# Moving four late modulation products and their weight loads from a block of their own into the attention-value loop, and storing the `ga` row as bf16

## The chip, the cores and the metric

The kernel runs on one core of one Trainium2 chip. The metric is the device time of one execution in microseconds (us). It was timed repeatedly. The profile is taken of one execution; its span is about 1.7 us shorter than that execution's time (773.4 against 775.11 us before).

Engines: PE does matmuls, PEld its weight loads, DVE is the vector engine, ACT the scalar engine, POOL the general one; SP only issues DMAs here. SBUF is the on-chip memory that holds the tiles, PSUM the one that PE writes its products to; a DMA is a transfer to or from DRAM.

## The reference, cut to what matters

An adaptive layer-norm transformer block, with 2048 tokens of width 1024. A conditioning vector `c` gives six modulation vectors; a sliding, dilated local attention (8 keys per query, 32 heads) and an MLP with mish activation follow.

```python
mod = (_silu(c) @ w_mod).reshape(c.shape[0], 6, 1, -1)      # w_mod: 1024 x 6144
sa, ca, ga, sb, cb, gb = (mod[:, i].copy() for i in range(6))
h = _layernorm(x) * (1 + ca) + sa
x = x + ga * _A_ref(h, A_wqkv, A_wo)       # local attention, then @ wo
h = _layernorm(x) * (1 + cb) + sb
x = x + gb * _B_ref(h, B_w1, B_b1, B_w2)   # MLP: 1024 -> 3584 -> 1024
```

`ca` and `sa` are wanted at the very start. `ga` is wanted when the attention output meets `wo`, `cb` and `sb` at the second layer norm, and `gb` only at the end. These four are the "late" vectors; their weights are 8 loads of 1 MB.

## The kernel before

Three stages: (1) Q and K projections, logits and softmax, token chunk by token chunk; the softmax weights (`attn`) go to DRAM. (2) For each of 32 items (4 chunks x 8 column blocks): project V (`emit_v`, PE), multiply by the softmax weights and half-sum (`emit_pv`, DVE), finish the sum with identity matmuls (`emit_osum`, PE). When a chunk is complete, multiply by `wo` (`emit_wo`, PE) and add the residual. (3) The MLP. The late modulation stood between (1) and (2), in what I call the seam:

```python
def emit_mod(i, late=False):
    j = mod_order[i]
    for e in range(NE):                                  # two halves of 512 columns
        ...
        mp = psum.tile([P, EC], FP32, name="mp", tag="mm", bufs=4)
        for kt in range(ND):                             # 8 matmuls; all 128 rows of mp are alike
            nc.tensor.matmul(mp[:], lhsT=silu_bc[:, kt, :], rhs=wm[:, kt, :], ...)
        if j in (SA, CA, SB_, CB):                       # take the diagonal: one value per partition
            ...
            nc.vector.tensor_mul(out=tmp[:, 0:NT, :], in0=mp[:]..., in1=ident[:]...)
            nc.vector.tensor_reduce(out=modT[:, j, ...], in_=tmp[:, 0:NT, :], axis=AX.X, op=ALU.add)
        elif j == GA:                                    # fold ga into the columns of wo
            row = wV.tile([P, EC], FP32, name="row", tag="x1", bufs=3)
            nc.vector.tensor_copy(out=row[:], in_=mp[:])
            for t in range(ND):
                nc.vector.tensor_mul(out=wo_sb[:, t, e * EC:(e + 1) * EC],
                                     in0=wo_sb[:, t, e * EC:(e + 1) * EC], in1=row[:])
        else:
            nc.vector.tensor_copy(out=gb_bc[:, e * EC:(e + 1) * EC], in_=mp[:])
...
workA.__exit__(None, None, None)          # stage 1's tiles (attn among them) give their memory up
...                                       # stage 2's pools (wV) take it
for k0 in range(n_first, n_hb, n_late_bufs):             # two rounds of four 1 MB loads
    for k in range(k0, min(n_hb, k0 + n_late_bufs)):
        nc.sync.dma_start(late_buf(k), wm_src(k))
    for k in range(k0, min(n_hb, k0 + n_late_bufs)):
        if (k - n_first) % NE == 0:
            emit_mod(k // NE, late=True)                 # GA, CB, then SB_, GB
... # first w1 loads, on the ACT queue

def emit_pv(ch, cb):
    for hf in range(NHALF):                              # two halves
        ...
        nc.vector.tensor_mul(out=pv, in0=attnB, in1=vwin)                        # 128x2048
        ... nc.vector.tensor_add(out=pv[:, :, 0:n, :], in0=..., in1=...)         # 128x1024
...
for it in range(n_items + 3):
    if it < n_items:
        ...
        emit_v(ch, cb)
    if 1 <= it <= n_items:
        emit_pv(*divmod(it - 1, ND))
    if 2 <= it <= n_items + 1:
        emit_osum(...)
    ...                                                  # emit_wo for chunk 0 from it = 10
```

The builder reorders what the program emits, engine by engine, so the order that runs is not quite the order of the text.

## Time and profile before

| kernel before | |
|---|---|
| timed | 776.07 us (median of 4 runs, 775.11 to 776.63) |
| span of the profile | 773.4 us |
| Q/K stage, then the seam, up to the first `wo` product | 0 to 239.15 us |
| first `wo` product to the end | 534.25 us |

The page of the kernel before opens with its span and each engine's busy time (share of the span, number of instructions):

```profile
span 773.4 us, 13166 instructions
## 1 busy us (share of the span) xinstructions
PE 718.9 (93%) x5297; PEld 439.2 (57%) x5378; DVE 571.0 (74%) x1004; ACT 446.1 (58%) x882; POOL 1.8 (0%) x9
```

PE looks like the only limit. That is an average, though. The timeline of DVE in the seam of the kernel before (columns: start us, length us, engine, line, operation, output <- inputs, count, and in brackets the idle time before it and what ended it):

```profile
176.79 1.29 DVE L352 TENSOR_REDUCE mx<-L_ps 128x128 f32<-128x512 f32 x2 [1.22 <-PE L_ps L339]
...
180.85 1.91 DVE L361 TENSOR_REDUCE sm<-Lsb 128x128 f32<-128x1024 f32 x1 [1.12 <-ACT Lsb L359]
182.79 0.95 DVE L362 RECIPROCAL sm<-sm 128x128 f32<-128x128 f32 x1
183.78 1.23 DVE L364 TENSOR_TENSOR attn<-Lsb,sm 128x1024 bf16<-128x1024 f32 x1
188.69 1.29 DVE L246 COPY row<-mp 128x512 f32<-128x512 f32 x2 [3.69 <-DMA attn_dram<-attn]
189.90 9.71 DVE L248 TENSOR_TENSOR arena<-arena,row 128x512 bf16<-128x512 bf16 x16
199.53 1.28 DVE L241 TENSOR_TENSOR diag_tmpL<-mp,ident 128x512 f32<-128x512 f32 x2
...
207.89 2.36 DVE L447 TENSOR_TENSOR arena<-attnB,vT 128x2048 bf16<-128x2048 bf16 x2 [1.65 <-ACT vT L434]
210.16 1.28 DVE L451 TENSOR_TENSOR arena<-arena 128x1024 bf16<-128x1024 bf16 x2
211.37 2.35 DVE L447 TENSOR_TENSOR arena<-attnB,vT 128x2048 bf16<-128x2048 bf16 x2
```

This is a serial chain. (`row` is the `ga` vector, copied out of PSUM; L246 is line 246 of the kernel.) The softmax of the last chunk runs until 185.0 us. DVE then stands 3.69 us idle until `attn` has landed in DRAM, because the first tile of stage 2 (`row`) takes memory that `attn` held. After that come the GA copies and 16 multiplies of `wo` (9.71 us), the diagonals, the `gb` copies. Only at 207.89 us does the first attention-value product (L447) start; from there an item takes about 3.48 us (207.89 to 211.37) with no idle. PE in the same seam, kernel before:

```profile
189.44 3.11 PE L233 MATMUL mp<-arena,silu_bc 128*128 128x512 bf16 x8 [3.29 <-DVE row L246]
...
200.26 2.72 PE L233 MATMUL mp<-arena,silu_bc 128*128 128x512 bf16 x6 [5.32 <-DVE diag_tmpL L241]
203.20 2.31 PE L233 MATMUL mp<-arena,silu_bc 128*128 128x512 bf16 x9 [0.22 <-issue]
205.34 5.34 PE L432 MATMUL mp<-hTv,arena 128*128 128x512 bf16 x24
...
239.15 0.38 PE L480 MATMUL mp<-arena,oT 128*128 128x512 bf16 x1
```

PE's modulation products (L233) wait for PSUM buffers that DVE frees, and the V projections (L432) come after all of them. The first `wo` product (L480) starts at 239.15 us. Between the last Q x K product on DVE (173.2 us) and that point, the table of stretches of the kernel before has (busy us of each engine, number of instructions, granted clock, DMA share and rate):

```profile
core 0: us, PE busy (x) PEld busy (x) DVE busy (x) ACT busy (x) POOL busy (x), PEclk, DMA share, GB/s
173.20:239.15 65.95, 47.62 (x248) 25.81 (x253) 57.62 (x75) 15.00 (x43) 0.00 (x0) 0.92 0.70 224
```

DVE works 57.62 of 65.95 us and idles 8.33; PE has 18 us to spare. So DVE is taken to be the limit of this stretch; after it, the same table has PE busy 519.11 of 534.25 us, so there PE is the limit. Lastly two lines of the table of groups of the kernel before (busy us, mean ns of one):

```profile
L451 DVE TENSOR_TENSOR arena<-arena 128x1024 bf16<-128x1024 bf16 x64 | 41.1, 682 | 0.0
L248 DVE TENSOR_TENSOR arena<-arena,row 128x512 bf16<-128x512 bf16 x16 | 9.7, 682 | 0.0
```

A multiply of `wo` with an fp32 `row` takes 682 ns for 512 elements; an all-bf16 add takes as long for twice as many.

### The profile page before, as it was taken

The numbers are of one execution on the slowest core, as the hardware profiler recorded it, in microseconds if no ns is written. First come the engines' busy times: TensorE is split into PE (matmuls) and PEld (weight loads), VectorE is DVE, ScalarE is ACT, GpSimd is POOL, SyncE is SP. The second block draws the span as 40 slices with busy tenths as digits, with TensorE's granted clock in tenths as the row PEclk, the third lists the DMA queues.
The fourth block names the chain that finished last, engine by engine and source line by source line (L and its number), as shares of the span: only waits on it lengthen the run. The fifth ranks groups of instructions, "written<-read, shape, count | busy, mean of one in ns | idle before, by whom it ended". The sixth has DMA issues, their size and how long they took to land.

```text
span 773.4 us, 13166 instructions
## 1 busy us (share of the span) xinstructions
PE 718.9 (93%) x5297; PEld 439.2 (57%) x5378; DVE 571.0 (74%) x1004; ACT 446.1 (58%) x882; POOL 1.8 (0%) x9
## 2 busy tenths in 40 slices
PE   2999999986779999999999999999999999999997
PEld 1444444442345555565677666767676666667653
DVE  3798875756899594951599978778777877778752
ACT  4387565430143879552489796685866757464520
POOL 0000000000000000000000000000000000000000
PEclk9999999998999999999999999999999999999999
DMA  9974212129913646159900312121020101101011
GB/s 325 369 286 164 70 56 69 56 62 319 321 54 115 219 153 195 63 171 300 345 1 25 94 29 88 42 76 42 21 69 28 35 28 35 42 21 42 22 48 48
DMA packets 52519, 87.90 MB, mean 114 GB/s; under 512 B 3690, under 2 KB 31338, under 8 KB 50794
## 3 DMA queue, kind: packets, MB, share of 16 engines
q1 hardware_dynamic: 44602, 75.52, 29.2%
q10 hardware_dynamic: 7856, 11.54, 4.4%
q8 instruction: 42, 0.69, 0.4%
q14 instruction: 19, 0.16, 0.1%
HBM read 69.22 MB, written 17.83 MB: 113 GB/s over the span
## 4 chain that ended last, share of the span: by engine, by line
PE 58%; DVE 23%; ACT 10%; DMA 5%; issue 3%; SPq 0%; DVEq 0%; another core or an unknown queue 0%; ACTq 0%
PE mp L585 22%; PE h L559 20%; DVE arena L447 6%; PE mp L312 6%; DVE arena L327 4%; PE mp L480 3%; DVE arena L451 3%; DMA xin<-in_A_x_dram 2%; DVE bn_st L150 2%; PE mp L233 2%; ACT ee L571 2%; PE mp L432 1%; DMA xres<-in_A_x_dram 1%; DVE arena L248 1%; ACT ee L572 1%
## 5 line engine op out<-in xcount | busy, mean ns | idle before, releaser
L559 PE MATMUL h<-h2T,arena 128*128 128x256 bf16 x1792 | 205.2, 273 | 0.3 <-DVE hm L564 0.2
L585 PE MATMUL mp<-arena,actT 128*128 128x512 bf16 x863 | 193.1, 379 | 2.4 <-DVE actT L576 0.6
L559 PEld LDWEIGHTS <-arena 128*128 128x128 bf16 x1792 | 174.3, 98 | 28.4 <-issue 2.4
L585 PEld LDWEIGHTS <-actT 128*128 128x128 bf16 x896 | 87.4, 98 | 99.5 <-DVE actT L576 1.8
L564 DVE TENSOR_SCALAR hm<-h,b1m 128x256 bf16<-128x256 f32 x224 | 99.6, 477 | 32.5 <-PE mp L483 21.2
L312 PE MATMUL mp<-hT,arena 128*128 128x512 bf16 x483 | 116.1, 379 | 2.1 <-issue 0.5
L571 ACT ACTIVATE ee<-ee,two_t 128x512 f32<-128x512 f32 x112 | 80.0, 716 | 44.4 <-DVE ee L570 44.3
L569 ACT ACTIVATE ee<-bigB 128x512 f32<-128x512 bf16 x112 | 69.0, 618 | 57.5 <-DVE bigB L567 56.7
L576 DVE SCALAR_TENSOR_TENSOR actT<-ee,hm 128x512 bf16<-128x512 f32 x112 | 76.9, 688 | 28.0 <-ACT ee L572 27.6
L327 DVE TENSOR_TENSOR arena<-qT,kT 128x2048 bf16<-128x2048 bf16 x64 | 75.6, 1212 | 28.7 <-ACT kT L317 28.7
L570 DVE SCALAR_TENSOR_TENSOR ee<-ee 128x512 f32<-128x512 f32 x112 | 76.8, 687 | 25.3 <-ACT ee L569 25.1
L447 DVE TENSOR_TENSOR arena<-attnB,vT 128x2048 bf16<-128x2048 bf16 x64 | 75.3, 1217 | 19.0 <-ACT vT L434 19.0
L312 PEld LDWEIGHTS <-arena 128*128 128x128 bf16 x512 | 47.0, 98 | 51.8 <-issue 0.7
L572 ACT ACTIVATE ee<-ee 128x512 f32<-128x512 f32 x112 | 69.7, 624 | 1.9
L432 PE MATMUL mp<-hTv,arena 128*128 128x512 bf16 x245 | 61.1, 379 | 0.5
L480 PE MATMUL mp<-arena,oT 128*128 128x512 bf16 x251 | 60.5, 379 | 0.3
L432 PEld LDWEIGHTS <-arena 128*128 128x128 bf16 x256 | 36.0, 144 | 16.0
L434 ACT CAST vT<-mp 128x512 bf16<-128x512 f32 x32 | 18.7, 586 | 45.1 <-PE mp L432 43.0
L462 PE MATMUL op<-arena,ident 128*128 128x256 bf16 x256 | 35.9, 273 | 7.7 <-DVE arena L451 6.5
L480 PEld LDWEIGHTS <-oT 128*128 128x128 bf16 x256 | 25.0, 98 | 28.9 <-issue 2.4
L451 DVE TENSOR_TENSOR arena<-arena 128x1024 bf16<-128x1024 bf16 x64 | 41.1, 682 | 0.0
L233 PE MATMUL mp<-arena,silu_bc 128*128 128x512 bf16 x93 | 27.4, 451 | 11.0 <-DVE diag_tmpL L241 5.3
(81 smaller groups left out, 555.5 us busy)
## 6 DMA issues: line engine op xcount, KB each, us to landing
arena<-in_w_mod_dram SPq DMA_DIRECT2D x8, 1024.0 KB, 7.3
x_dram<-x SPq DMA_DIRECT2D x32, 256.0 KB, 3.0
x1c<-x_dram SPq DMA_DIRECT2D x16, 512.0 KB, 3.7
bigB<-x_dram SPq DMA_DIRECT2D x32, 256.0 KB, 3.0
arena<-in_B_w_dram ACTq DMA_DIRECT2D x7, 1024.0 KB, 6.7
arena<-in_B_w_dram SPq DMA_DIRECT2D x4, 1792.0 KB, 9.2
xin<-in_A_x_dram SPq DMA_DIRECT2D x16, 256.0 KB, 6.2
arena<-in_w_mod_dram SPq DMA_DIRECT2D x2, 2048.0 KB, 11.2
```

The source lines that it names most:

```text
L312: nc.tensor.matmul(mp[:], lhsT=wqk_sb[:, which, kt, cb * P:(cb + 1) * P], rhs=hT[:, kt, :], start=(kt == 0), stop=(kt == ND - 1))
L327: nc.vector.tensor_mul(out=prod, in0=qT[:, hf * SH:(hf + 1) * SH].unsqueeze(1).to_broadcast([P, W, SH]), in1=_ap(kT[:, HALO + hf * SH:HALO ...
L432: nc.tensor.matmul(mp[:], lhsT=wqk_sb[:, 2, kt, bass.ds(cb, P, step=ND)], rhs=hTv[:, kt, :], start=(kt == 0), stop=(kt == ND - 1))
L447: nc.vector.tensor_mul(out=pv, in0=attnB, in1=vwin)
L480: nc.tensor.matmul(mp[:], lhsT=oT[:, cb, b * P:(b + 1) * P], rhs=wo_sb[:, cb, e * EC:(e + 1) * EC], start=(cb == 0), stop=False)
L559: nc.tensor.matmul(mp[:, i, :], lhsT=w1_sb[:, ft // 4, kt, (ft % 4) * P:(ft % 4 + 1) * P], rhs=h2T[:, kt, :], start=(kt == 0), stop=(kt == ...
L564: nc.vector.tensor_scalar(out=hm2[:, i, :], in0=mp[:, i, :], scalar1=-2.0, scalar2=b1m2[:, ft:ft + 1], op0=ALU.mult, op1=ALU.add)
L570: nc.vector.scalar_tensor_tensor(out=ee[:], in0=ee[:], scalar=2.0, in1=ee[:], op0=ALU.add, op1=ALU.mult)
L571: nc.scalar.activation(out=ee[:], in_=ee[:], func=ACT.Ln, bias=two_t[:], scale=1.0)
L572: nc.scalar.activation(out=ee[:], in_=ee[:], func=ACT.Exp, scale=-1.0)
L576: nc.vector.scalar_tensor_tensor(out=halves[ft0 // NFH][:, ft0 % NFH:ft0 % NFH + 2, :], in0=ee[:], scalar=0.5, in1=hm2[:], op0=ALU.subtrac ...
L585: nc.tensor.matmul(mp[:], lhsT=actT_of(ch, ft)[:, b * P:(b + 1) * P], rhs=w2_sb[:, ft, e * EC:(e + 1) * EC], start=(ft == 0), stop=(ft == ...
```

## The change

Its intent is to hide the weight loads and the modulation products behind the V loop: the four late vectors are emitted one by one in loop steps 1, 2, 4 and 5, their loads in steps 0 and 3, and the first `w1` loads in step 6. `row` becomes bf16 and moves to another ring (the buffers that tiles of one `tag` take in turn).

```diff
-                row = wV.tile([P, EC], FP32, name="row", tag="x1", bufs=3)
+                row = wV.tile([P, EC], BF16, name="row", tag="xres", bufs=3)
...
-    for k0 in range(n_first, n_hb, n_late_bufs):
-        for k in range(k0, min(n_hb, k0 + n_late_bufs)):
-            nc.sync.dma_start(late_buf(k), wm_src(k))
-        for k in range(k0, min(n_hb, k0 + n_late_bufs)):
-            if (k - n_first) % NE == 0:
-                emit_mod(k // NE, late=True)
...
+    late_sched = {}
+    n_late_vec = (n_hb - n_first) // NE
+    vec_per_round = max(1, n_late_bufs // NE)
+    itc = 0
+    for v0 in range(0, n_late_vec, vec_per_round):
+        vecs = list(range(v0, min(n_late_vec, v0 + vec_per_round)))
+        late_sched.setdefault(itc, []).append(("load", vecs))
+        for vv in vecs:
+            itc += 1
+            late_sched.setdefault(itc, []).append(("mod", vv))
+        itc += 1
+    late_sched.setdefault(itc, []).append(("w1", None))
+    def emit_late(it): ...      # emits the loads, emit_mod(2 + vv, late=True) or the w1 loads of this step
...
-    for it in range(n_items + 3):
+    for it in range(max(n_items + 3, max(late_sched) + 1)):
         ch, cb = divmod(it, ND)
+        emit_late(it)
```

More of the change, by code (lines that the diff above doesn't have):

```diff
@@ L396, with emit_late @@
     wV = workV.__enter__()
-    for k0 in range(n_first, n_hb, n_late_bufs):
-        for k in range(k0, min(n_hb, k0 + n_late_bufs)):
-            nc.sync.dma_start(late_buf(k), wm_src(k))
-        for k in range(k0, min(n_hb, k0 + n_late_bufs)):
-            if (k - n_first) % NE == 0:
-                emit_mod(k // NE, late=True)
     w1_v = B_w1.rearrange("(t p) (g n) -> p g t n", p=P, n=EC)
     n_early = min(NG1, (2 * ND * D) // (ND * EC))
-    for g1 in range(NG1):
-        if g1 < n_early or g1 * ND * EC >= NQK:
-            nc.scalar.dma_start(w1_sb[:, g1], w1_v[:, g1])
+    late_sched = {}
[10 more added lines that the diff above has]
+    late_sched.setdefault(itc, []).append(("w1", None))
+    def emit_late(it):
+        for kind, arg in late_sched.get(it, []):
+            if kind == "load":
+                for vv in arg:
+                    for e in range(NE):
+                        k = n_first + vv * NE + e
+                        nc.sync.dma_start(late_buf(k), wm_src(k))
+            elif kind == "mod":
+                emit_mod(2 + arg, late=True)
+            else:
+                for g1 in range(NG1):
+                    if g1 < n_early or g1 * ND * EC >= NQK:
+                        nc.scalar.dma_start(w1_sb[:, g1], w1_v[:, g1])
     oT_tiles = {}
```

## The prediction

> **What bounds the kernel now.** PE is busy 93% of the span (engine table), and 287.5 of the 289 us from 450 to 739. The change touches one seam, between the last Q/K projection (172.5 us) and the first attention-value product (L447, 207.9 us). In the table of stretches, 168 to 206 us has PE 25.4, DVE 28.5, ACT 3.3 of 38 us. The timeline shows a serial chain on DVE: last softmax (176.8 to 185.0), 3.7 us of waiting for the attn write to DRAM, then 188.7 to 206.2 the GA row copies (1.3), 16 multiplies of wo (9.7), diagonal extraction and gb copies. PE's mod products wait for PSUM buffers that DVE frees (5.3 and 3.3 us). V projections come after all of them, so the first pv starts 1.65 us after DVE has run dry. Then items 0 to 8 of the V loop are DVE-bound at 3.475 us each, until wo joins at 239.2 us and PE is the limit (76.9 of 80 us).
>
> **What the change does.** The built order shows V0 ahead of the mod products, pv of items 0 and 1 inside the last softmax, GA after attn, then CB; SB after pv 2, gb after pv 3; from pv 5 on every engine has the order of before. So only the seam can change, and what counts is DVE time from 173.2 us to the end of pv 8.
>
> 1. DVE idle filled: 1.2 (before mx), 1.1 (before sm), 0.5 (gb), 1.65 (first pv): 4.5 us.
> 2. The row becomes bf16. The Trainium skill, "VectorE: DVE Perf Modes", walkthrough of mode 2x_1P, asks 16-bit operands for two results a cycle. Trace: L248 with an fp32 row takes 682 ns for 512 elements (0.607 us start to start); L451, all bf16, 682 ns for 1024 (0.60). I estimate 415 ns, 0.34 us start to start: 16 times 0.27 = 4.3 us less.
> 3. Not removed: the built row copy still waits for the DMA lanes of the attn write (landing 3.7 us); only one add (0.6 us) stands between attn and it. About 3 us of idle remain.
> 4. New stalls: first pv on vT (0.7), gb on PE through the 4-buffer PSUM ring (0.5).
>
> Sum by hand over the built order: attn done at 190, row at 193.6, wo multiplies 200.3, CB 202.8, SB 209, gb 214, pv 8 ends 231.5 instead of 239.2: 7.7 us. PE needs about 37 us in these 56 and should not bind.
>
> **Critical path.** All 7.7 us lie on it: DVE-bound up to wo, then PE-bound with unchanged order and work, so of unchanged length.
>
> **Prediction.** 776.1 - 7.7 = 768.3 us, range 765.5 to 772. Faster by over 2%: 0.04; within 2%: 0.95; slower by over 2%: 0.01.
>
> **What would show it.** L248's mean falls from 682 to about 415 ns (group table); the first wo product (L480) starts near 231.5 us; DVE idle from 173 to 231 us is 4 to 5 us, most of it the row's wait on the attn write; from the first wo product to the end stays 534 us within 1 us.
>
> **What would make it wrong.** L248 not speeding up (772.5); the row not waiting for the attn write (765.5); PE stalls on PSUM or w_mod loads starving pv; a bottleneck downstream, such as the xres waits at 360 to 373 us beside the w2 load, swallowing the shift.

## The result

| | before | after |
|---|---|---|
| timed, median (lowest to highest) | 776.33 us (775.05 to 776.84, 13 runs) | 765.77 us (765.03 to 769.11, 8 runs) |
| ratio | | 0.9872, 95% interval 0.9861 to 0.9884 |
| span of the profile | 773.4 us | 764.1 us |

A ratio is the mean time of one kernel's runs over that of the other's of the same rounds, so it is not quite the ratio of the medians quoted. 1 - 0.9872 of 776.3 us is 9.9 us; the medians differ by 10.6, the spans by 9.3. It is 1.3%, well clear of noise. The prediction was 7.7 us.

The page of the changed kernel opens with:

```profile
span 764.1 us, 13172 instructions
PE 716.3 (94%) x5297; PEld 439.2 (57%) x5378; DVE 566.1 (74%) x1004; ACT 445.8 (58%) x882; POOL 1.8 (0%) x9
```

DVE in the seam, changed kernel (line numbers have shifted: L447 is now L464, L451 is L468, L432 is L449, L480 is L497):

```profile
176.34 1.22 DVE L464 TENSOR_TENSOR arena<-attnB,vT 128x2048 bf16<-128x2048 bf16 x1 [0.66 <-ACT vT L451]
177.49 1.28 DVE L352 TENSOR_REDUCE mx<-L_ps 128x128 f32<-128x512 f32 x2
...
189.37 0.68 DVE L468 TENSOR_TENSOR arena<-arena 128x1024 bf16<-128x1024 bf16 x1
192.72 1.29 DVE L246 CAST row<-mp 128x512 bf16<-128x512 f32 x2 [2.67 <-DMA attn_dram<-attn]
193.93 5.44 DVE L248 TENSOR_TENSOR arena<-arena,row 128x512 bf16<-128x512 bf16 x16
199.29 1.28 DVE L241 TENSOR_TENSOR diag_tmpL<-mp,ident 128x512 f32<-128x512 f32 x2
...
211.08 1.27 DVE L251 CAST gb_bc<-mp 128x512 bf16<-128x512 f32 x2
212.28 2.34 DVE L464 TENSOR_TENSOR arena<-attnB,vT 128x2048 bf16<-128x2048 bf16 x2
214.55 1.28 DVE L468 TENSOR_TENSOR arena<-arena 128x1024 bf16<-128x1024 bf16 x2
```

Attention-value products now fill the holes of the softmax, the wait on the `attn` write is still there but 2.67 us long, the 16 multiplies take 5.44 us instead of 9.71, and `gb` is followed by the loop at once. PE, changed kernel:

```profile
184.50 1.90 PE L233 MATMUL mp<-arena,silu_bc 128*128 128x512 bf16 x8 [0.68 <-DMA arena<-in_w_mod_dram]
193.47 3.57 PE L449 MATMUL mp<-hTv,arena 128*128 128x512 bf16 x8 [7.07 <-DVE row L246]
...
229.63 0.38 PE L497 MATMUL mp<-arena,oT 128*128 128x512 bf16 x1
```

PE has a new wait of 7.07 us, for the PSUM buffer that the GA copy frees, but DVE's idle time does not come from it: of DVE's 3.61 us of idle in this stretch, 2.67 are the row's wait and 0.66 and 0.25 stand before it. The first `wo` product starts at 229.63 us instead of 239.15. The same stretch in the changed kernel, from the last Q x K product to that point (columns as above):

```profile
173.30:229.63 56.33, 44.28 (x247) 25.52 (x252) 52.72 (x75) 14.80 (x43) 0.00 (x0) 0.94 0.81 263
```

DVE's busy time fell from 57.62 to 52.72 us and its idle time from 8.33 to 3.61 (56.33 - 52.72). Together that is 9.6 us, which is the whole gain of the profile: from the first `wo` product to the end both kernels take the same time, 534.25 us before and 764.1 - 229.63 = 534.47 after. The group of the multiplies, changed kernel:

```profile
L248 DVE TENSOR_TENSOR arena<-arena,row 128x512 bf16<-128x512 bf16 x16 | 5.4, 415 | 0.0
```

### The profile page after: what moved, and what is told of

It reads as the page before. It is cut to its first block, busy times and chain, and to the rows that moved or that the text cites. A ratio compares the mean times of both kernels' runs of the same rounds, so it can differ in the third digit from the quotient of the medians.

```text
span 764.1 us, 13172 instructions
## 1 busy us (share of the span) xinstructions
PE 716.3 (94%) x5297; PEld 439.2 (57%) x5378; DVE 566.1 (74%) x1004; ACT 445.8 (58%) x882; POOL 1.8 (0%) x9
## 4 chain that ended last, share of the span: by engine, by line
PE 57%; DVE 23%; ACT 11%; DMA 5%; issue 3%; SPq 1%; DVEq 0%; another core or an unknown queue 0%; ACTq 0%
PE mp L602 22%; PE h L576 20%; PE mp L312 6%; DVE arena L464 6%; DVE arena L327 4%; PE mp L497 3%; DVE arena L468 2%; ACT ee L588 2%; DVE bn_st L150 2%; DMA xin<-in_A_x_dram 2%; PE mp L449 1%; ACT ee L589 1%; DMA xres<-in_A_x_dram 1%; PE mp L233 1%; DVE actT L593 1%
## 5 line engine op out<-in xcount | busy, mean ns | idle before, releaser
L464 DVE TENSOR_TENSOR arena<-attnB,vT 128x2048 bf16<-128x2048 bf16 x64 | 75.5, 1216 | 18.2 <-ACT vT L451 18.2
L449 PE MATMUL mp<-hTv,arena 128*128 128x512 bf16 x245 | 62.7, 388 | 7.5 <-DVE row L246 7.1
L497 PE MATMUL mp<-arena,oT 128*128 128x512 bf16 x251 | 60.4, 379 | 0.2
L449 PEld LDWEIGHTS <-arena 128*128 128x128 bf16 x256 | 36.1, 144 | 25.0 <-issue 8.8
L451 ACT CAST vT<-mp 128x512 bf16<-128x512 f32 x32 | 18.7, 585 | 44.7 <-PE mp L449 41.7
L497 PEld LDWEIGHTS <-oT 128*128 128x128 bf16 x256 | 24.9, 98 | 28.9 <-issue 2.3
L468 DVE TENSOR_TENSOR arena<-arena 128x1024 bf16<-128x1024 bf16 x64 | 41.2, 681 | 0.0
L528 ACT ACTIVATE h2T<-tpB,modT 128x256 bf16<-128x256 bf16 x64 | 32.7, 559 | 8.6 <-PE tpB L525 8.6
```

Source lines behind the costliest of these rows:

```text
L449: nc.tensor.matmul(mp[:], lhsT=wqk_sb[:, 2, kt, bass.ds(cb, P, step=ND)], rhs=hTv[:, kt, :], start=(kt == 0), stop=(kt == ND - 1))
L497: nc.tensor.matmul(mp[:], lhsT=oT[:, cb, b * P:(b + 1) * P], rhs=wo_sb[:, cb, e * EC:(e + 1) * EC], start=(cb == 0), stop=False)
```

## The experiments

Two theories stand against each other.

- **Theory A:** the seam is bound by DVE's time. The gain is DVE time taken out (the bf16 row) plus DVE idle filled (the interleaving).
- **Theory B:** the gain is what the change is meant for: weight loads and products on PE hidden behind the V loop. The dtype of `row` is a side show.

The table lists all runs in one view: the stretch from the last Q x K product on DVE to the first `wo` product, from the table of stretches of each run's profile, beside the timed result. "Idle" is length minus busy time.

| run | timed median, us | ratio to before | stretch, us | DVE busy | DVE idle | PE busy |
|---|---|---|---|---|---|---|
| before | 776.33 | 1 | 65.95 | 57.62 | 8.33 | 47.62 |
| the change | 765.77 | 0.9872 | 56.33 | 52.72 | 3.61 | 44.28 |
| e1_fp32_row | 770.10 | 0.9927 | 60.50 | 56.95 | 3.55 | 45.39 |
| e2_bf16_row_only | 773.40 | 0.9974 | 63.80 | 53.34 | 10.46 | 47.53 |
| e2_again | 772.89 | 0.9960 | 65.00 | 53.30 | 11.70 | 46.05 |
| e3_row_free | 763.27 | 0.9843 | 53.23 | 52.57 | 0.66 | 43.04 |
| e4_more_pe | 767.17 | 0.9889 | 56.40 | 52.84 | 3.56 | 50.01 |
| e5_copies_on_act | 760.54 | 0.9792 | 50.99 | 50.28 | 0.71 | 43.23 |
| e6_wo_on_pool | 768.24 | 0.9893 | 58.40 | 57.70 | 0.70 | 45.34 |
| e7_both | 767.86 | 0.9884 | 58.70 | 56.74 | 1.96 | 45.47 |
| e8_loads_on_act_queue | 774.63 | 0.9966 | 63.60 | 53.21 | 10.39 | 46.35 |

Each experiment was timed beside the kernel before in five rounds on one chip; the medians of before in those three batches were 775.98 (e1 to e4), 777.17 (e5 to e7) and 777.21 us (e8, e2_again). All results are correct. After the stretch, the profiled executions differ too, from 533.61 us (e5_copies_on_act) to 536.29 (e2_again), so a difference in the stretch need not come through in full.

### e1_fp32_row: the interleaving alone

```diff
-                row = wV.tile([P, EC], BF16, name="row", tag="xres", bufs=3)
+                row = wV.tile([P, EC], FP32, name="row", tag="x1", bufs=3)
```

> The changed kernel with the row put back to fp32 (old slot): DVE order is built the same, each L248 is back to about 682 ns. Theory A (the seam is bound by DVE time, and the bf16 row is worth its 16 x 0.27 us = 4.3 us there): 765.8 + 4.3 = 770.1 us, first wo product at 233.9 us. Theory B (the gain is the earlier V projections and the hidden weight loads on PE; the row's dtype is a side show): 766 to 767 us.

Measured: 770.10 us, as theory A had it. DVE in the seam of e1_fp32_row:

```profile
192.55 1.29 DVE L246 COPY row<-mp 128x512 f32<-128x512 f32 x2 [2.67 <-DMA attn_dram<-attn]
193.75 9.71 DVE L248 TENSOR_TENSOR arena<-arena,row 128x512 bf16<-128x512 bf16 x16
```

The wait of the row is the same 2.67 us as in the changed kernel, the multiplies take 9.71 us again, and 60.50 - 56.33 = 4.2 us of the stretch come back. The row's dtype is worth 4.3 us once the interleaving is there (770.10 - 765.77). The edit also moves `row` to another ring of tiles; that this is not the cause is seen in e3, where the bf16 row lies in a third ring and one multiply takes 0.42 us.

### e2_bf16_row_only: the bf16 row alone

The kernel before with the reverse of e1's edit.

> The kernel before with only the row made bf16 (no interleaving): instruction order as before on DVE, ACT, SP. Theory A: DVE's serial chain in the seam is 4.3 us shorter, 776.3 - 4.3 = 772.0 us, first wo product near 234.9 us. Theory B: 775.5 to 776.5 us.

Measured: 773.40 us, a gain of only 2.6 us over the 775.98 of the same batch (ratio 0.9974), with a wide spread, 771.7 to 776.7. It lies between the two theories. In the profile DVE's busy time did fall by 4.3 us (57.62 to 53.34), but its idle time rose by 2.1 (8.33 to 10.46): 1.0 us before the maxima of the last softmax (2.20 instead of 1.22), 0.4 before the second `gb` copy and 0.7 before the first attention-value product. e8 and a repetition, below, look for the cause.

### e3_row_free: the wait on the write of attn

```diff
-                row = wV.tile([P, EC], BF16, name="row", tag="xres", bufs=3)
+                row = small.tile([P, EC], BF16, name="row", tag="mx", bufs=2)
```

`mx` holds the softmax maxima; its ring is free of the write to DRAM.

> The changed kernel with the row (bf16) in the ring of the softmax maxima, which the write of attn to DRAM does not hold; the builder then moves the row copies and wo multiplies ahead of attn. Theory A: the 2.7 us in which DVE waited for that write are filled, 765.8 - 2.7 = 763.1 us. Theory B: no change, since PE has the same work and loads, 765.5 to 766.3 us.

Measured: 763.27 us; theory A had 763.1, theory B no change. DVE in e3_row_free:

```profile
178.56 0.68 DVE L246 CAST row<-mp 128x512 bf16<-128x512 f32 x1
179.36 0.42 DVE L248 TENSOR_TENSOR arena<-arena,row 128x512 bf16<-128x512 bf16 x1
...
194.35 1.28 DVE L241 TENSOR_TENSOR diag_tmpL<-mp,ident 128x512 f32<-128x512 f32 x2
```

The GA copy and the multiplies now stand inside the softmax. By my reading of the built order, which no trace shows, the wait on the `attn` write has passed to the first diagonal (194.35 us); its line shows no idle time before it. DVE's idle time is down to 0.66 us. The stretch is 3.1 us shorter than in the changed kernel (56.33 - 53.23), but what follows it is 1.2 us longer in this execution (762.1 - 226.43 = 535.67 against 534.47): there PE waits 4.1 us in all for loads of `xres` (the rows of `x` for the residual), against 2.6 us in the changed kernel. This is the risk downstream that the prediction names.

### e4_more_pe: more work for PE

```diff
-            for kt in range(ND):
+            xt = list(range(ND // 2)) if late else []
+            for q, kt in enumerate(xt + list(range(ND))):
                 nc.tensor.matmul(mp[:], lhsT=silu_bc[:, kt, :], rhs=wm[:, kt, :],
-                                 start=(kt == 0), stop=(kt == ND - 1))
+                                 start=(kt == 0), stop=(kt == ND - 1 or q == len(xt) - 1))
```

> The changed kernel with four throw-away matmuls ahead of each late mod product: 32 x 0.216 = 6.9 us more PE in the seam, DVE work unchanged, result unchanged. Theory A: PE has 49 of 61.5 us busy there, so most is hidden: 765.8 plus 0 to 2 us. Theory B: about 765.8 + 6.9 = 772.7 us.

Measured: 767.17 us (765.71 to 768.32), 1.4 us above the change. The profiled execution is the fastest of the four (765.71), so no trace shows where the 1.4 us go. The stretch of e4_more_pe (columns as above):

```profile
173.10:229.50 56.40, 50.01 (x279) 28.62 (x284) 52.84 (x75) 14.88 (x43) 0.00 (x0) 0.97 0.82 259
```

PE is busy 50.01 us instead of 44.28, and the stretch is 56.40 us instead of 56.33. Theory B, which had 6.9 us more, falls for the changed kernel as far as PE's time goes; the weight loads are not tested here. (The builder moved a few DVE instructions around for the longer products; DVE's idle time is 3.56 us in all, against 3.61.)

### e8_loads_on_act_queue and e2_again: where the bf16 row's gain went without the interleaving

e8 is e2 with the late loads issued from the ACT queue:

```diff
-            nc.sync.dma_start(late_buf(k), wm_src(k))
+            nc.scalar.dma_start(late_buf(k), wm_src(k))
```

> e2 (the kernel before with only the bf16 row) gained 2.6 us where theory A had 4.3; in its trace the last gb product waited 1.9 us for its w_mod load, which sat in the SP queue behind the attn writes. This is e2 with the eight late w_mod loads issued from the ACT queue. If that load held the rest of the gain back: the wait goes, and the time is 1 to 2 us below e2's, about 771.5 to 772.5 us. If not (for instance a slower clock of PE in the seam): as e2.

> e2 again, on the same chip as e8 for comparison: 773.4 us as before, if its 2.6 us were no accident of that chip.

Measured: e2_again 772.89 us, as the first time, with the same spread (771.74 to 776.67); e8 774.63 us. My expectation for e8 was a miss. Against the kernel before of its own batch (777.21 us), e2_again gains 4.3 us by the medians, which is theory A's figure, and 3.1 by the ratio (0.9940 to 0.9980), where the first e2 had 2.6 and 2.0. So the timed runs leave open whether any of the 4.3 us is missing; the traces show DVE waiting more in the executions profiled. That of e2_again was one of its long ones (776.37 us, granted clock 0.998). Of its 2.9 us over the profile of the first e2 only 1.2 lie in the stretch; 2.2 lie after it (536.29 against 534.09 us), and 0.5 fewer before it. PE and then DVE in e2_again:

```profile
201.08 3.37 PE L233 MATMUL mp<-arena,silu_bc 128*128 128x512 bf16 x8 [3.27 <-DMA arena<-in_w_mod_dram]
```

```profile
204.49 0.69 DVE L251 CAST gb_bc<-mp 128x512 bf16<-128x512 f32 x1 [3.78 <-PE mp L233]
207.05 2.36 DVE L447 TENSOR_TENSOR arena<-attnB,vT 128x2048 bf16<-128x2048 bf16 x2 [1.87 <-ACT vT L434]
```

The last modulation product waits 3.27 us for its 1 MB load, DVE waits 3.78 us for that product and then 1.87 us more for the first V projection, which stands behind it on PE. The load is not all of it: the product itself takes 3.37 us at a granted PE clock of 0.66 (mean of 200 to 205 us), where the first e2 took 1.90 for the same eight matmuls at 1.00, after a wait of 1.89 us for the load. In e8 that wait is gone, but not the time:

```profile
192.58 1.29 DVE L246 CAST row<-mp 128x512 bf16<-128x512 f32 x2 [6.48 <-DMA attn_dram<-attn]
...
203.99 1.28 DVE L251 CAST gb_bc<-mp 128x512 bf16<-128x512 f32 x2
205.88 2.36 DVE L447 TENSOR_TENSOR arena<-attnB,vT 128x2048 bf16<-128x2048 bf16 x2 [0.61 <-ACT vT L434]
```

`gb` follows without idle and the first product of the loop waits 0.61 us only. In exchange the wait of `row` on the `attn` write grew from 3.7 to 6.48 us. So in these traces, with the multiplies shortened and no interleaving, DVE waits for a DMA somewhere in the seam whichever of the two queues issues the 8 MB of late weights. That the `attn` write landed later in e8 because it shared the DMA engines with loads that had moved ahead of it is my reading; it fits that from 185 to 190 us they moved 348 GB/s in e8 and 201 in the first e2, but no run took those loads away. The changed kernel does not have this limit: SB and GB come several V items later, and DVE waits for no modulation product in its seam. Here theory B may have its share; no run shows how much of the time it is.

### e5_copies_on_act: less work for DVE

e3, and the four copies of `row` and `gb` go to ACT:

```diff
-                nc.vector.tensor_copy(out=row[:], in_=mp[:])
+                nc.scalar.copy(out=row[:], in_=mp[:])
...
-                nc.vector.tensor_copy(out=gb_bc[:, e * EC:(e + 1) * EC], in_=mp[:])
+                nc.scalar.copy(out=gb_bc[:, e * EC:(e + 1) * EC], in_=mp[:])
```

> e3 with the two row copies and the two gb copies moved from DVE to ACT (ACT is busy 15 of 53 us there). If DVE still bounds the seam, it loses four copies of 0.60 us start to start: 763.3 - 2.4 = 760.9 us. If PE or the loads have taken over, 763 us.

Measured: 760.54 us, ratio 0.9792 (0.9774 to 0.9810). This version beats both kernels. Its stretch, e5_copies_on_act (columns as above):

```profile
173.40:224.39 50.99, 43.23 (x248) 25.05 (x253) 50.28 (x71) 17.04 (x47) 0.00 (x0) 1.00 0.89 288
```

DVE is busy 50.28 of 50.99 us; the stretch shrank by 2.2 us against e3, for four copies of about 0.6 us each. DVE is still the limit, with PE at 43.23. By the ratios e5 gains 4.0 us on e3 (0.9843 - 0.9792), by the medians 2.7; the two were timed on different chips, and 2.1 us of the profiles' difference lie after the stretch (535.67 against 533.61), so only the 2.2 us of the stretch are put down to the copies.

### e6_wo_on_pool and e7_both: the multiplies on POOL

e6 is e3 with the 16 multiplies of `wo` on POOL, which otherwise idles; e7 is e5 and e6 together.

```diff
-                    nc.vector.tensor_mul(out=wo_sb[:, t, e * EC:(e + 1) * EC], ...
+                    nc.gpsimd.tensor_mul(out=wo_sb[:, t, e * EC:(e + 1) * EC], ...
```

> e3 with the 16 wo multiplies moved from DVE to POOL, which idles (wo is wanted only some 30 us later). If DVE bounds the seam and POOL does not slow it: 763.3 - 5.4 = 757.9 us, DVE busy about 47 us up to the first wo product. If POOL's multiplies are too slow to be done by then (over 2 us each) or lengthen DVE's own instructions, less: 760 to 765 us.

> e5 and e6 together: 763.3 - 7.8 = 755.5 us if DVE bounds the seam to the end. PE needs 43 us in what would then be 45 us, so I expect a part to be lost to PE: 755.5 to 758 us.

Measured: 768.24 and 767.86 us, both misses. By its ratio e6 is about 4 us slower than e3 (0.9893 against 0.9843) instead of 5.4 us faster. POOL and DVE in e6_wo_on_pool:

```profile
179.32 26.95 POOL L248 TENSOR_TENSOR arena<-arena,row 128x512 bf16<-128x512 bf16 x16 [176.83 <-DVE row L246]
```

```profile
180.95 1.28 DVE L357 TENSOR_TENSOR Lsb<-L_ps,mx 128x512 f32<-128x512 f32 x2
...
186.63 1.41 DVE L468 TENSOR_TENSOR arena<-arena 128x1024 bf16<-128x1024 bf16 x1
...
190.06 2.17 DVE L364 TENSOR_TENSOR attn<-Lsb,sm 128x1024 bf16<-128x1024 f32 x1
...
193.71 4.25 DVE L464 TENSOR_TENSOR arena<-attnB,vT 128x2048 bf16<-128x2048 bf16 x2
...
205.18 1.27 DVE L241 TENSOR_TENSOR diag_tmpL<-mp,ident 128x512 f32<-128x512 f32 x2
...
217.74 2.35 DVE L464 TENSOR_TENSOR arena<-attnB,vT 128x2048 bf16<-128x2048 bf16 x2
```

POOL works from 179.3 to 206.3 us. In that time two attention-value products (L464) take 4.25 us on DVE instead of 2.35, the `attn` multiply 2.17 instead of 1.21, and one add (L468) 1.41 instead of 0.68; after it the pair takes 2.35 us again. The instructions with one operand in PSUM are not stretched: the subtraction of the maxima (L357) takes 1.28 us and the diagonals (L241) 1.27, as in the changed kernel. DVE's busy time in the stretch is 57.70 us instead of 52.57, so moving 5.4 us of work off DVE added 5.1. The Trainium skill, "SBUF — State Buffer", section "Who interferes with whom", says why: a DVE instruction with two inputs in SBUF contends with a POOL instruction that reads SBUF, because its second input comes through a read interface that the two engines share; one with at most one SBUF input, outside the two-port performance modes, does not. The trace agrees with both points; how the two take turns at the interface, it does not show. The expectation had named the possibility only as an "if"; the page would have told beforehand that they contend.

## Why the prediction was right

**The limit.** "what counts is DVE time from 173.2 us to the end of pv 8." Right. That DVE's busy and idle time add up to the stretch shows nothing by itself, as they do so for any engine. What shows it are the experiments: e4 shows that PE has slack there, and e1, e3 and e5 that DVE time put back or taken out of the stretch (4.2, 3.1 and 2.2 us) shows in the time (4.3, 2.5 and 2.7 us by the medians, the last across two chips). Two rivals were not given a run of their own. The DMA engines moved 14.8 MB in the stretch of both kernels (224 GB/s for 65.95 us, 263 for 56.33); at the 348 GB/s that they reached in the kernel before from 195 to 200 us, I estimate 42.5 us for that, less than DVE's busy time in any run. And PE's granted clock fell to 0.66 in both (200 to 205 us before, where DVE waits for PE; 190 to 200 us in the changed kernel, where it does not), so a part of the idle time before, such as the 0.50 and 1.65 us of the waits for `gb` and the first V projection, may be due to a slowed PE.

**The row.** Predicted 415 ns for one multiply and 4.3 us in all; measured 415 ns, and 9.71 against 5.44 us. e1 gives 4.3 us in the timed runs. The rate agrees with the Trainium skill, "VectorE: DVE Perf Modes", mode 2x_1P: one fp32 operand of three was enough to hold the instruction at the slow rate.

**Everything else** was under-sized. The gain was 9.9 us by the ratio (10.6 by the medians) where 7.7 had been predicted, and 765.77 us lies only 0.3 us above the lower end of the stated range, 765.5. The prediction had tied that end to the row not waiting for the `attn` write. The row did wait, so the time alone would have pointed to the wrong cause. The hand sum had 7.7 - 4.3 = 3.4 us for the interleaving; the traces show 9.6 - 4.3 = 5.3, and e1 alone, timed, 5.9 us (775.98 - 770.10). Three terms, from the two timelines: the row's remaining wait is 2.67 us, not about 3.1; the expected stall of 0.5 us before `gb` did not come; and 0.67 us is DVE busy time (overlapping instructions are counted once) that vanishes by order alone (57.62 in before, 56.95 in e1, with the same instructions). In before, each step of the last softmax depends on the one before: the reciprocal starts at 182.79 us, after the sum has ended (180.85 + 1.91). In the changed kernel independent instructions stand between, and one starts some 0.08 us before the other ends (176.34 + 1.22 = 177.56, the next starts at 177.49). I had used that start-to-start spacing for the multiplies and the loop, but plain durations for the softmax. These three make 1.6 of the 1.9 us; the rest stays open. Two more figures were off for the same stretch: DVE's idle time is 3.6 us, not 4 to 5, and PE is busy 44.28 us where "about 37" had been reckoned, which still left it slack.

**The row's wait on the `attn` write** was predicted to survive, and it did; e3 shows that another place for one tile removes it, for 2.5 us by the medians (765.77 - 763.27).

**Downstream.** "from the first wo product to the end stays 534 us within 1 us": 534.25 and 534.47. No swallowing here; in the profile of e3 a wait downstream did take 1.2 us back.

**What the prediction did not see** is that its two halves seem to lean on each other. In the stretch of the traces the interleaving alone takes out 65.95 - 60.50 = 5.45 us, the bf16 row alone 2.15 (e2) or 0.95 us (e2_again), and both together 9.62. Without the interleaving, part of what the bf16 row takes from DVE's work comes back in these traces as DVE waiting, for a DMA or for PE. In the timed runs this is not clear of noise: the ratios of the halves add up to 0.73% + 0.26 or 0.40%, against 1.28% for both, and the interval of e2 alone (0.9954 to 0.9994) is as wide as the difference. The prediction was about both together, so its number was not hurt.

## What to carry to other kernels

Where a kernel is bound by PE nearly everywhere, look for the stretch where it is not, and count the busy and idle time of the engine that binds there: here a 66 us stretch bound by DVE gave the whole gain, and two later steps (another ring for one tile, four copies to ACT) could be sized from the same two numbers. The dtype of a small helper operand can matter nearly as much as the reordering that a change is named after (here 4.3 against 5.9 us). And a move to an idle engine can cost more than it saves: here 5.4 us of multiplies moved to POOL saved nothing, as DVE was busy 5.1 us longer in the stretch.

## What the Trainium skill lacked or had wrong

- "VectorE: DVE Perf Modes", "The perf-mode tier table", lists bf16, fp32 and PSUM operands for `tensor_tensor`, but no mixed case. Here bf16 x fp32 to bf16, all in SBUF, took 682 ns for 512 elements, and 415 ns with all three in bf16. (The rule in "What auto-detection actually checks" does cover it: every tensor has to be 16-bit.)
- "SBUF — State Buffer", "Who interferes with whom", was right, but has no figure for a `tensor_tensor` on each side. Here five of six DVE products of 128x2048 bf16 took about 2.1 us (the sixth 1.3) instead of 1.2 while POOL multiplied 128x512 tiles, and those took 1.1 to 2.1 us each, against 0.415 us of the same multiply on DVE.
